# Converting weight pieces from a single load, with the low part made on GpSimd and the first units reordered

## The chip, the cores and the metric

The kernel runs on one core of a Trainium2 chip. The core has a matrix engine (PE, whose weight loads the profile lists apart as PEld), a vector engine (DVE), an activation engine (ACT), GpSimd (POOL) and SyncE (SP), which here issues nearly all transfers. The metric is device time in microseconds (us) of one execution; lower is better. All times below are us unless marked ns.

## The reference

Two stages follow each other. The first is attention with random-feature maps; its output is regrouped to 4608 rows of 512, and a feed-forward layer is applied to it.

```python
def phi(x):                                   # q, k, v: (8, 8, 576, 64); w_phi: (64, 128)
    proj = np.einsum('bhsd,df->bhsf', x, w_phi)
    proj = proj - np.max(np.abs(proj), axis=-1, keepdims=True)
    return np.concatenate([np.exp(proj), np.exp(-proj)], axis=-1)
q_p, k_p = (phi(q), phi(k))
kv = np.einsum('bhsf,bhsd->bhfd', k_p, v)
num = np.einsum('bhsf,bhfd->bhsd', q_p, kv)
den = np.einsum('bhsf,bhf->bhs', q_p, np.sum(k_p, axis=2))[..., None] + 1e-06
...
h = x @ w_in                                  # x: (4608, 512), w_in: (512, 2048)
sp = np.where(h > 20.0, h, np.log1p(np.exp(np.minimum(h, 20.0))))
out = (h * np.tanh(sp)) @ w_out               # w_out: (2048, 512)
```

The two weight matrices `w_in` and `w_out` arrive as 8-byte numbers (float64) and have to be turned into 4-byte ones on the chip.

## The kernel before

**Attention units.** The keys come as 36 units k0, k1, ... and the queries as 36 units q0_0, q0_1, q1_0, ... of 512 columns each. A unit is loaded (`load k0`, tile `raw`), projected on PE (`project`, L360, tiles `pp`), has its absolute maxima taken and subtracted on DVE (`centre`, L364 and L372: two reductions and two subtractions, one of each per half), and goes through the exponential on ACT. A key unit is then summed against the values `v` on PE (`sum`, L401, tiles `kvps`). A query unit is first turned (`dt`, L480, in its first three groups by PE), multiplied with the key sums (`num`, L401), divided on DVE (`divide`, L523 to L525, three instructions), turned back (`xt`, L545) and split into a high and a low part (`xTh` on ACT, `xTl` on DVE).

**Feed-forward.** For each group c of 256 rows PE multiplies `x` with `w_in` (`in c f`, L575, tiles `h`), ACT applies the nonlinearity, and PE multiplies with `w_out` (`out c f`, L610, tiles `o`; from the fifth group on in a form with fewer products, L745). Each product is the sum of three, high x high, high x low and low x high, so every weight piece is needed as a high tile and a low tile.

**Weight pieces.** Both matrices are cut into 32 pieces of 128 x 512 numbers, named `("in", i, j)` and `("out", i, 0)`. `win_2_0` is the converted piece ("in", 2, 0). A piece is loaded as raw words (`words`, L256), and a second load (`middle`, L260) brings the same bytes shifted by two bytes, for all but the last three pieces. From the high word ACT takes the magnitude (`abs`, L265). DVE then clamps it (L279), shifts it (L292) and puts back sign and top bits (L297), which gives the high part; from the shifted load it makes the remaining bits (L284) and a power of two (L302), and multiplies the two to the low part (L307). ACT rounds the high part to its final tile (`ready`, L326). So DVE works six instructions on a piece with a shifted load, and seven on one of the last three (L287 and L288 take the place of L284).

**What sets the order.** Every step is a task with an engine, a key, a guessed duration and dependencies. `Plan.order` replays them and so writes down one fixed order for PE, DVE, ACT and SP; each engine then takes its instructions strictly in this order and waits where an input is late. The keys come from tables of numbers at the top (`FIRST_KEYS` and `FIRST_QUERIES` for the first units, `WKEYS` for the weight pieces, E0, E1 and others for the steady stretch). Behind the replay the first loads are rearranged by hand (NLOADS, VLATE, LATER). Transfers share one issue order on SP, and the hardware takes them from there.

The raw words and the finished piece use the same memory: the finished high tile overwrites part of the words.

Of the kernel before, what the change touches and what calls it, by code (L numbers as in the profile page):

```python
# [57 lines left out]
FIRST_KEYS = {0: -15.83, 1: -13.11, 2: -9.97, 3: -9.13, 4: -7.79, 5: 5.39, 6: 7.33, 7: 10.36, 8: 12.26, 9: 26.17, 10: 26.27}  # L58
FIRST_QUERIES = {0: -11.55, 1: -8.5, 2: -1.4, 3: -0.74, 4: 12.74, 5: 12.11}
# [11 lines left out]
WKEYS = [-6.42, -8.84, -5.8, -0.77, 4.55, 2.54, 6.13, 9.34, 4.27, 5.56, 11.66, 11.19, 18.21, 21.9, 23.26, 22.05,  # L71
         25.09, 22.07, 26.7, 34.84, 24.54, 37.47, 32.85, 40.81, 37.93, 41.3, 40.78, 41.2, 43.66, 37.64, 39.51, 45.36]
LAG, TAIL, TAILLAG = 4, 10, 2
TWOH = 10
HFIRST = 0.0
# [4 lines left out]
TLEAD = 3.609  # L80
SPLITC = 12
QFIRST = 99
URGENT = 2.061
UCENTRE = -0.136
# [4 lines left out]
class Plan:  # L89
# [11 lines left out]
    def order(self):  # L101
# [86 lines left out]
        at = [n for n, task in enumerate(tasks) if task["name"].startswith("load ")][:NLOADS]  # L188
        loads = sorted(range(NLOADS), key=lambda i: i + VLATE * tasks[at[i]]["name"].startswith("load v"))
        for n, task in zip(at, [tasks[at[i]] for i in loads]):  # L190
            tasks[n] = task
        moved = [next(task for task in tasks if task["name"] == name) for name in LATER]
        tasks = [task for task in tasks if task["name"] not in LATER]
        at = 1 + next(n for n, task in enumerate(tasks) if task["name"] == LATER_THAN)
        return tasks[:at] + moved + tasks[at:]
# [3 lines left out]
def attention_then_mish(ctx, tc, qT, kT, va, w_phi, w_in, w_out, out):  # L199
# [24 lines left out]
    weight, finished, homes_of, to_add, middles, rests = {}, {}, {}, {}, {}, {}  # L224
# [42 lines left out]
    def parts_of(piece):  # L267
        words = weight[piece].rearrange("p (a b) -> p a b", b=2)
        if piece in middles:
            return words, middles[piece].bitcast(U32).rearrange("p (a b) -> p a b", b=2)  # L270
        if piece not in rests:
            nm = "%s_%d_%d" % piece
            rests[piece] = (scratch(f"rest_{nm}", f"rest:{piece}", U32),
                            work.tile([P, 512], U32, tag="half", name=f"t_{nm}", bufs=NHALF))
        return words, None

# [4 lines left out]
    def split_rest(piece):  # L281
        words, middle = parts_of(piece)
        if middle is not None:
            nc.vector.tensor_scalar(middle[:, :, 0], middle[:, :, 0], 7, None, op0=ALU.logical_shift_left)  # L284
        else:
            rest = rests[piece][0]
            nc.vector.tensor_scalar(rest, words[:, :, 1], 23, None, op0=ALU.logical_shift_left)  # L287
            nc.vector.scalar_tensor_tensor(rest, words[:, :, 0], 9, rest, op0=ALU.logical_shift_right, op1=ALU.bitwise_or)  # L288
# [5 lines left out]
    def split_sign(piece):  # L294
        w = to_add[piece]
        words = weight[piece].rearrange("p (a b) -> p a b", b=2)
        nc.vector.scalar_tensor_tensor(w, words[:, :, 1], 0xC0000000, w, op0=ALU.bitwise_and, op1=ALU.bitwise_or)  # L297

    def split_power(piece):
        words, middle = parts_of(piece)  # L300
        t = rests[piece][1] if middle is None else middle[:, :, 1]
        nc.vector.tensor_scalar(t, to_add[piece], 0xFF800000, None, op0=ALU.bitwise_and)  # L302

    def split_low(piece):
        _, middle = parts_of(piece)
        rest, t = rests[piece] if middle is None else (middle[:, :, 0], middle[:, :, 1])
        nc.vector.scalar_tensor_tensor(both(piece)[1], like(piece, rest), 2.0 ** -43, like(piece, t.bitcast(F32)),  # L307
                                       op0=ALU.mult, op1=ALU.mult)
# [15 lines left out]
    def high_weight(kind, i, j):  # L324
        piece = kind, i, j
        nc.scalar.copy(both(piece)[0], like(piece, to_add.pop(piece).bitcast(F32)))  # L326
# [532 lines left out]
    for t, is_query, n in units:  # L859
# [5 lines left out]
        if not is_query:  # L865
# [12 lines left out]
            for k, (p, parts) in enumerate(mine):  # L878
# [75 lines left out]
    nmiddle = len(pieces) - len(homes)  # L954
    for i, pc in enumerate(pieces):
# [5 lines left out]
        if i < nmiddle:  # L961
            home = homes[i % len(homes)]
            add(f"middle {nm}", "SP", -47.45 + i * 0.1, 0.42, lambda pc=pc, home=home: load_middle(*pc, home),
                deps=last_use.get(home, []), take=[(home, f"m:{nm}")], size=524288)
# [203 lines left out]
```

## Time and profile before

| What | Value |
|---|---|
| Three timed runs | 1046.14 us median (1042.16 to 1047.18) |
| Profiled execution, first to last instruction | 1043.5 us |
| Profiled execution's own time | no figure apart from its span; the median of the runs lies 2.6 us above the span |
| PE busy | 1029.5 us, 99% of the span |
| DVE busy | 738.0 us, 71% |
| ACT busy | 655.6 us, 63% |
| POOL busy | 0.7 us, 6 instructions |
| Moved by transfers | 223.09 MB |

The shares are means over an opening of some 170 us, in which the weights are converted, and a long steady stretch. They differ between the two, so the opening has to be looked at by itself.

### The profile page before, as it was taken

What the parts mean: (1) busy time and instruction counts of PE and PEld (TensorE: products, weight loads), DVE (VectorE), ACT (ScalarE), POOL (GpSimd) and SP (SyncE); (2) the same over time, 40 slices, a digit from 0 to 9 for tenths busy, and PEclk for the clock granted to TensorE, in tenths of its full rate; (3) what the DMA queues carried; (4) which work ended last, traced back from release to release, by engine and by line L of the source; (5) the groups of instructions that cost most, each with busy time, mean ns of one, the idle gap of its engine ahead of it and who ended that gap; (6) DMA issues with size and microseconds to landing.
All of it is one profiled execution on the core that took longest, in us unless ns stands there. A gap on an engine that the chain in (4) does not pass through costs nothing.

```text
span 1043.5 us, 30075 instructions
## 1 busy us (share of the span) xinstructions
PE 1029.5 (99%) x12286; PEld 990.6 (95%) x12286; DVE 738.0 (71%) x1692; ACT 655.6 (63%) x1028; POOL 0.7 (0%) x6
## 2 busy tenths in 40 slices
PE   8999999999999999999999999999999999999998
PEld 7888998899889999999999999999999999999998
DVE  7998998677886675767676767675776666666553
ACT  6799898667665756666666656665665565545532
POOL 0000000000000000000000000000000000000000
PEclk9999999999999999999999999999999999999999
DMA  9768664465977666767667564757576666765844
GB/s 319 271 235 317 189 209 136 125 204 160 296 246 235 212 211 205 222 215 226 216 209 230 193 209 159 242 186 243 175 237 196 206 189 212 219 220 190 291 142 155
DMA packets 158313, 223.09 MB, mean 214 GB/s; under 512 B 17120, under 2 KB 75616, under 8 KB 158176
## 3 DMA queue, kind: packets, MB, share of 16 engines
q1 hardware_dynamic: 158032, 221.11, 64.8%
q8 instruction: 97, 1.59, 0.6%
q14 instruction: 40, 0.33, 0.1%
q10 hardware_dynamic: 144, 0.07, 0.0%
HBM read 177.59 MB, written 43.52 MB: 212 GB/s over the span
## 4 chain that ended last, share of the span: by engine, by line
PE 93%; DVE 3%; DMA 3%; issue 1%; SPq 1%; ACT 0%; DVEq 0%; ACTq 0%
PE h L575 38%; PE oy L745 8%; PE ox L745 8%; PE o L610 8%; PE ow L745 8%; PE num L401 7%; PE kvps L401 6%; PE oz L745 4%; PE pp_q L360 4%; PE pp_k L360 3%; DMA middle_in<-w_in 1%; DMA words_out<-w_out 1%; DMA v<-va 1%; DMA words_in<-w_in 0%; PE dt L480 0%
## 5 line engine op out<-in xcount | busy, mean ns | idle before, releaser
L575 PE MATMUL h<-xTh,win 128*128 128x256 f32 x2304 | 429.1, 280 | 1.0 <-DVE e_k L372 1.0
L575 PEld LDWEIGHTS h<-xTh,win 128*128 128x128 f32 x2304 | 361.0, 188 | 5.2 <-PE h L575 1.2
L575 PE MATMUL h<-xTl,win 128*128 128x256 f32 x1152 | 321.9, 279 | 0.0
L575 PEld LDWEIGHTS h<-xTl,win 128*128 128x128 f32 x1152 | 216.5, 188 | 1.8
L660 DVE TENSOR_TENSOR sl<-s,sh 128x640 fp32r<-128x640 f32 x112 | 92.0, 823 | 106.7 <-ACT sh L656 101.7
L656 ACT CAST sh<-s 128x640 fp32r<-128x640 f32 x112 | 80.7, 722 | 90.8 <-DVE s L651 79.2
L641 ACT ACTIVATE u<-h 128x512 f32<-128x512 f32 x112 | 66.9, 598 | 96.2 <-PE h L575 95.7
L649 DVE TENSOR_TENSOR s<-u 128x256 f32<-128x256 f32 x112 | 46.9, 418 | 90.5 <-ACT u L641 90.3
L401 PEld LDWEIGHTS kvps<-v,e_k 128*64 128x64 f32 x2560 | 78.4, 137 | 9.4 <-issue 4.2
L401 PE MATMUL kvps<-v,e_k 128*64 128x66 f32 x2560 | 84.0, 223 | 3.2 <-issue 2.5
L745 PE MATMUL oy<-wout,sh 128*128 128x256 f32 x448 | 85.7, 284 | 0.0
L745 PE MATMUL ox<-wout,gh 128*128 128x256 f32 x440 | 83.6, 283 | 0.0
L745 PE MATMUL ow<-wout,sh 128*128 128x256 f32 x440 | 82.9, 281 | 0.0
L610 PE MATMUL o<-wout,gh 128*128 128x512 f32 x256 | 81.7, 400 | 0.0
L401 PE MATMUL num<-kv,e_q 128*64 128x66 f32 x2304 | 78.1, 225 | 1.8 <-DVE xTl L559 1.0
L401 PEld LDWEIGHTS num<-kv,e_q 128*64 128x64 f32 x2304 | 73.2, 139 | 4.9 <-issue 1.5
L436 ACT ACT_TABLE_LOAD x25 | 32.1, 1283 | 64.9 <-DVE e_k L372 64.5
L745 PEld LDWEIGHTS oy<-wout,sh 128*128 128x128 f32 x448 | 68.5, 188 | 1.6
L745 PEld LDWEIGHTS ox<-wout,gh 128*128 128x128 f32 x440 | 67.2, 188 | 0.7
L745 PEld LDWEIGHTS ow<-wout,sh 128*128 128x128 f32 x440 | 67.4, 188 | 0.0
L745 PE MATMUL oy<-wout,sl 128*128 128x256 f32 x224 | 62.9, 281 | 0.0
L745 PE MATMUL ow<-wout,sl 128*128 128x256 f32 x220 | 61.7, 280 | 0.0
(120 smaller groups left out, 1824.4 us busy)
## 6 DMA issues: line engine op xcount, KB each, us to landing
wout<-terms SPq DMA_DIRECT2D x344, 256.0 KB, 4.6
there_e<-e_q SPq DMA_DIRECT2D x60, 256.0 KB, 2.6
e_q<-there_e SPq DMA_DIRECT2D x240, 64.0 KB, 2.3
v<-va SPq DMA_DIRECT2D x32, 330.0 KB, 4.8
out<-osb SPq DMA_DIRECT2D x35, 256.0 KB, 2.6
raw_k<-kT SPq DMA_DIRECT2D x34, 256.0 KB, 3.5
raw_q<-qT SPq DMA_DIRECT2D x34, 256.0 KB, 3.5
there_x<-via SPq DMA_DIRECT2D x30, 256.0 KB, 2.0
```

The source lines that it names most:

```text
L360: nc.tensor.matmul(ps[j][:, n], raw[rows, n * P:(n + 1) * P], w_phi2[rows], start=True, stop=True)
L401: nc.tensor.matmul(ps[rows], lhsT[h], rhs[h], start=start, stop=stop, skip_group_check=True)
L436: nc.scalar.activation(e[:, 1, :], e[:, 0, :], AF.Exp)
L575: nc.tensor.matmul(ps, w[:, wcol], x[:, cc % 2, :], start=(n == 0), stop=(n == 11))
L610: nc.tensor.matmul(ps.rearrange("p (k n) -> p k n", k=2), g[:, cols], w, start=(i == first and k == 0), stop=(i == end and k == 2))
L641: nc.scalar.activation(u, h_live.pop((c, fp)).rearrange("p f s -> p (f s)"), AF.Mish)
L649: nc.vector.tensor_tensor(s[:, :CH], u[:, :CH], u[:, CH:], op=ALU.add)
L656: nc.scalar.copy(mix_high[c, fp], mixed[c, fp])
L660: nc.vector.tensor_sub(mix_low[c, fp], mixed.pop((c, fp)), mix_high[c, fp].bitcast(F32))
L745: nc.tensor.matmul(ps, a, b, start=(begins and n == 0 and (apart or not half)), stop=(ends and n == 2), skip_group_check=True)
```

## The change

The second, shifted load is gone (29 transfers of 511.5 KB), and with it L284, L302 and L307 on DVE (for the last three pieces also L287 and L288). The high word keeps 9 more bits through the shift, and one new DVE instruction, `tail`, adds the top three bits of the low word. ACT then rounds this fuller number to the high tile, and GpSimd subtracts the high tile from the fuller number, which gives the low tile. DVE is left with four instructions for a piece. GpSimd's instructions are now ordered by the plan too. The key tables and the steady stretch's numbers are others, the hand-made rearrangement of loads is removed, and a dependency keeps the sums of a pair of heads in the order of their units.

```diff
-EARLY = 2.042
+EARLY = 1.984
-SOONER = 1.5
+SOONER = 1.602
-FIRST_KEYS = {0: -15.83, 1: -13.11, 2: -9.97, 3: -9.13, 4: -7.79, 5: 5.39, 6: 7.33, ...
+FIRST_KEYS = {0: -18.68, 1: -15.48, 2: -11.31, 3: -9.5, 4: -6.98, 5: -5.65, 6: 5.13, ...
-NLOADS = 11
-LATER = ["load ('in', 0, 1)", "load ('out', 0, 0)", "load ('out', 2, 0)", "load ('out', 3, 0)"]
-LATER_THAN = "load v5"
-VLATE = 4.5
-E0 = 0.138
-E1 = 0.171
-GX = 0.403
-ET = 0.107
+E0 = -1.33
+E1 = -1.113
+GX = 0.577
+ET = 0.456
-URGENT = 2.061
-UCENTRE = -0.136
+URGENT = 3.619
+UCENTRE = -1.189
...
-    def load_middle(kind, i, j, home):
-        middle = middles[kind, i, j] = slot_tile(home, U16, f"middle_{kind}_{i}_{j}", 2048)
-        in_parts(middle[:, :2046], octets(kind, i, j).bitcast(U16)[:, 1:2047])
...
-    def split_rest(piece):
...
     def split_shift(piece):
         w = to_add[piece]
-        nc.vector.tensor_scalar(w, w, 3, 0x3FFFF000, op0=ALU.logical_shift_left, op1=ALU.bitwise_and)
+        nc.vector.tensor_scalar(w, w, 3, 0x3FFFFFF8, op0=ALU.logical_shift_left, op1=ALU.bitwise_and)
...
+    def split_or(piece, half, scalar, op):
         w = to_add[piece]
         words = weight[piece].rearrange("p (a b) -> p a b", b=2)
+        nc.vector.scalar_tensor_tensor(w, words[:, :, half], scalar, w, op0=op, op1=ALU.bitwise_or)
+    def split_sign(piece):
+        split_or(piece, 1, 0xC0000000, ALU.bitwise_and)
+    def split_tail(piece):
+        split_or(piece, 0, 29, ALU.logical_shift_right)
     def split_low(piece):
-        nc.vector.scalar_tensor_tensor(both(piece)[1], like(piece, rest), 2.0 ** -43, like(piece, t.bitcast(F32)),
-                                       op0=ALU.mult, op1=ALU.mult)
+        hi, lo = both(piece)
+        nc.gpsimd.tensor_sub(lo, like(piece, to_add.pop(piece).bitcast(F32)), hi.bitcast(F32))
...
-        split("power", 0.34, split_power, [f"sign {nm}", f"rest {nm}" if own else f"middle {nm}"])
-        split("split", 0.61, split_low, [f"power {nm}", f"rest {nm}"], ...
+        split("tail", 0.61, split_tail, [f"sign {nm}"])
+        add(f"ready {nm}", "ACT", WKEYS[i] + 0.1, 0.55, lambda pc=pc: high_weight(*pc), deps=[f"tail {nm}"])
+        add(f"split {nm}", "POOL", WKEYS[i] + 0.2, 1.4, lambda pc=pc: split_low(pc), deps=[f"ready {nm}"], give=[f"u:{nm}", f"w:{nm}"])
```

Line numbers shift with the edit: in the changed kernel L317 loads a unit (L352 before), L396 loads `v` (L431), L240 loads a piece (L251), L254, L258 and L263 are the clamp, the shift, and the two instructions `sign` and `tail` (L279, L292, L297), and L273 is the subtraction.

**SP, the start of the program.** These are the first transfers that SP issues before the change; a `raw` tile holds two units, so the first three rows are units k0, k1 and q0_0.

```order
L352 DMA raw_k0_89<-kT 128x128 x4
L352 DMA raw_k0_89<-kT 128x512
L352 DMA raw_q0_0_95<-qT 128x512
L352 DMA raw_q0_0_95<-kT 128x512
L431 DMA v_0_98<-va 128x660
```

The same place in the changed kernel:

```order
L317 DMA raw_k0_89<-kT 128x128 x4
L396 DMA v_0_94<-va 128x660
L317 DMA raw_k0_89<-kT 128x512
L396 DMA v_1_97<-va 128x660
L317 DMA raw_q0_0_99<-qT 128x512
```

The value tiles v_0 and v_1 have moved ahead of units k1 and q0_0, so that k1 has one more transfer in front of it and q0_0 two.

**DVE, ahead of the first feed-forward product.** Before the change these rows are the end of the work on piece ("in", 3, 0), the last of the four pieces that the first `in` needs, with the centring of query unit q1_1 and the division of q1_0 around it.

```order
L284 TENSOR_SCALAR middle_in_3_0_508<-middle_in_3_0_508 128x512
L297 SCALAR_TENSOR_TENSOR w_in_3_0_629<-words_in_3_0_159,w_in_3_0_629 128x512
L559 TENSOR_TENSOR xTl_0_1_725<-xt_0_1_707,xTh_0_1_715 128x512
L302 TENSOR_SCALAR middle_in_3_0_508<-w_in_3_0_629 128x512
L364 TENSOR_REDUCE m0_q1_1_730<-pp0_q1_1_611 128x4
L364 TENSOR_REDUCE m1_q1_1_732<-pp1_q1_1_612 128x4
L372 TENSOR_TENSOR e0_q1_1_734<-pp0_q1_1_611,m0_q1_1_730 128x512
L372 TENSOR_TENSOR e1_q1_1_736<-pp1_q1_1_612,m1_q1_1_732 128x512
L307 SCALAR_TENSOR_TENSOR win_3_0_738<-middle_in_3_0_508 128x512
L523 TENSOR_SCALAR r0_1_0_785<-num0_1_0_740 128x4
```

In the changed kernel the last of these four pieces is ("in", 2, 0); L254 is its clamp, L258 its shift, and the two L263 rows are sign and tail.

```order
L254 TENSOR_SCALAR w_in_2_0_619<-w_in_2_0_619 128x512
L436 COPY kv_4_733<-kvps_4_646 128x264
L258 TENSOR_SCALAR w_in_2_0_619<-w_in_2_0_619 128x512
L254 TENSOR_SCALAR w_out_0_0_692<-w_out_0_0_692 128x512
L263 SCALAR_TENSOR_TENSOR w_in_2_0_619<-words_in_2_0_125,w_in_2_0_619 128x512
L524 TENSOR_TENSOR xTl_0_1_756<-xt_0_1_724,xTh_0_1_740 128x512
L263 SCALAR_TENSOR_TENSOR w_in_2_0_619<-words_in_2_0_125,w_in_2_0_619 128x512
L258 TENSOR_SCALAR w_out_0_0_692<-w_out_0_0_692 128x512
```

The rows on `middle` and the multiplication into `win` are gone from DVE, the piece's fourth and last step is a second L263, and steps of ("out", 0, 0) stand between them; the centring of q1_1 follows behind these rows. The subtraction that ends the piece is no longer here: GpSimd, which had nothing behind the identity matrix at the start, now has 32 rows L273, one for each piece, each behind ACT's rounding of its piece.

**PE, behind the products of query unit q0_1.** Before the change the first half of q0_1's `num` is followed by the projections of q1_0 and q1_1 (rows that repeat are left out).

```order
L401 MATMUL num0_0_1_568<-kv_2_565,e0_q0_1_348 64x66 x4
L401 MATMUL num0_0_1_568<-kv_2_565,e1_q0_1_350 64x66 x4
L360 MATMUL pp0_q1_0_596<-w_phi2_80,raw_k4_105 128x128
L360 MATMUL pp1_q1_0_597<-w_phi2_80,raw_k4_105 128x128
L360 MATMUL pp0_q1_1_611<-w_phi2_80,raw_q1_1_196 128x128
L360 MATMUL pp1_q1_1_612<-w_phi2_80,raw_q1_1_196 128x128
```

In the changed kernel the same `num` is followed by the projection of key unit k5, and those of q1_0 and q1_1 come behind it.

```order
L366 MATMUL num0_0_1_542<-kv_2_536,e0_q0_1_348 64x66 x4
L366 MATMUL num0_0_1_542<-kv_2_536,e1_q0_1_350 64x66 x4
L325 MATMUL pp0_k5_563<-w_phi2_80,raw_k4_155 128x128
L325 MATMUL pp1_k5_564<-w_phi2_80,raw_k4_155 128x128
L325 MATMUL pp0_q1_0_583<-w_phi2_80,raw_q1_0_197 128x128
L325 MATMUL pp1_q1_0_584<-w_phi2_80,raw_q1_0_197 128x128
```

The projection of k5, and behind it the sums of k5 (80 products in the trace's count), have moved ahead of the first feed-forward product; before the change both stand behind the fourth.

## Rows read from the trace of the kernel before

**Rows 1.** Page, part 1: busy time, share of the span, instructions of each engine.

```profile
PE 1029.5 (99%) x12286; PEld 990.6 (95%) x12286; DVE 738.0 (71%) x1692; ACT 655.6 (63%) x1028; POOL 0.7 (0%) x6
```

**Rows 2.** Windows: length, busy time by engine (instructions), PE's granted clock, DMA share, GB/s.

```profile
0.00:46.69 46.69, 40.00 (x747) 36.74 (x747) 38.08 (x85) 30.39 (x63) 0.70 (x6) 0.96 0.88 308
0.00:73.75 73.75, 65.47 (x1123) 60.40 (x1123) 63.79 (x143) 55.44 (x102) 0.70 (x6) 0.98 0.79 273
0.00:100.00 100.00, 91.52 (x1360) 82.79 (x1362) 87.73 (x198) 80.20 (x153) 0.70 (x6) 0.98 0.82 284
170.00:1000.00 830.00, 827.89 (x9832) 804.36 (x9832) 566.74 (x1301) 501.99 (x761) 0.00 (x0) 1.00 0.66 212
```

**Rows 3.** Timeline, DVE: start, length, line, operation, count, idle time before.

```profile
5.17 1.29 DVE L364 TENSOR_REDUCE m_k<-pp_k 128x4 f32<-128x512 f32 x2 [5.17 <-PE pp_k L360]
6.37 1.28 DVE L372 TENSOR_TENSOR e_k<-pp_k,m_k 128x512 f32<-128x512 f32 x2
...
18.27 0.43 DVE L284 TENSOR_SCALAR middle_in<-middle_in 128x512 uint32<-128x512 uint32 x1 [1.46 <-DMA middle_in<-w_in]
...
23.15 0.42 DVE L279 TENSOR_SCALAR w_in<-w_in 128x512 f32<-128x512 f32 x1
23.48 0.42 DVE L284 TENSOR_SCALAR middle_in<-middle_in 128x512 uint32<-128x512 uint32 x1
...
27.30 1.29 DVE L307 SCALAR_TENSOR_TENSOR win<-middle_in 128x512 fp32r<-128x512 uint32 x2
28.51 0.68 DVE L364 TENSOR_REDUCE m_k<-pp_k 128x4 f32<-128x512 f32 x1
...
44.61 0.15 DVE L523 TENSOR_SCALAR r<-num 128x4 f32<-128x4 f32 x1
...
45.35 0.42 DVE L279 TENSOR_SCALAR w_out<-w_out 128x512 f32<-128x512 f32 x1
```

**Rows 4.** Timeline, PE: the opening's products that the sum counts.

```profile
5.70 2.08 PE L360 MATMUL pp_k<-w_phi,raw_k 64*128 64x128 f32 x16 [0.57 <-DMA raw_k<-kT]
...
26.69 1.16 PE L360 MATMUL pp_k<-w_phi,raw_k 64*128 64x128 f32 x16
...
28.37 2.56 PE L401 MATMUL kvps<-v,e_k 128*64 128x66 f32 x80
30.76 1.11 PE L401 MATMUL num<-kv,e_q 128*64 128x66 f32 x32
...
40.68 0.60 PE L401 MATMUL num<-kv,e_q 128*64 128x66 f32 x6 [0.98 <-DVE xTl L559]
...
46.25 0.60 PE L480 MATMUL dt<-ident,e_q 128*128 128x128 f32 x4
...
46.69 0.60 PE L545 MATMUL xt<-ident,x 128*128 128x128 f32 x4
...
73.75 0.73 PE L610 MATMUL o<-wout,gh 128*128 128x512 f32 x2
```

**Rows 5.** Chain that ended last: start, length, engine, tile, line, count.

```profile
205.74 2.80 PE o L610 x12
```

**Rows 6.** Groups by line, ACT and POOL: count, busy, mean ns, idle before.

```profile
L326 ACT CAST win<-w_in 128x512 fp32r<-128x512 f32 x16 | 9.9, 626 | 1.4 <-DVE w_in L297 1.4
masks.py:199 POOL TENSOR_SCALAR_AFFINE_SELECT ident<-ident 128x128 f32<-128x128 f32 x1 | 0.3, 294 | 0.1
L641 ACT ACT_TABLE_LOAD x45 | 57.7, 1283 | 0.8
```

**Rows 7.** Windows again: the stretch of the slower clock, and the first loads.

```profile
40.00:45.00 5.00, 4.32 (x70) 4.19 (x71) 4.87 (x13) 2.49 (x5) 0.00 (x0) 0.66 1.01 385
...
4.00:6.00 2.00, 1.43 (x14) 1.14 (x12) 0.83 (x2) 0.00 (x0) 0.00 (x0) 1.00 0.97 316
```

More of the change, by code (lines that the diff above doesn't have):

```diff
@@ L187, in order @@
         tasks = [task for _, _, task in issued]
[L188 to L195, printed above, removed]
+        return tasks
 @with_exitstack
@@ L223, in attention_then_mish @@
     pieces += [("out", 12 + i, 0) for i in range(4)]
-    weight, finished, homes_of, to_add, middles, rests = {}, {}, {}, {}, {}, {}
+    weight, finished, homes_of, to_add = {}, {}, {}, {}
     slots = [f"w{kind}_{i}_{j}" for kind, i, j in pieces]
@@ L265, in magnitude @@
         nc.scalar.activation(w.bitcast(F32), high.bitcast(F32), AF.Abs)
[L267 to L275, printed above, removed]
     def split_clamp(piece):
@@ L957, in attention_then_mish @@
         ahead = [f"split {pieces[i - NAHEAD]}"] if i >= NAHEAD else []
-        used = [f"split {pieces[n]}" for n in range(nmiddle) if homes[n % len(homes)] == slot]
         add(f"load {nm}", "SP", -47.5 + i * 0.1, 0.42, lambda pc=pc: load_weight(*pc),
-            deps=last_use.get(slot, []) + used, after=ahead, take=[(slot, f"w:{nm}")], size=524288)
[L961 to L964, printed above, removed]
+            deps=last_use.get(slot, []), after=ahead, take=[(slot, f"w:{nm}")], size=524288)
         add(f"abs {nm}", "ACT", WKEYS[i] - 0.5, 0.55, lambda pc=pc: magnitude(*pc), deps=[f"load {nm}"], take=[("w", f"u:{nm}"), ("part", f"w:{nm}")])
@@ L967, in split @@
             add(f"{step} {nm}", "DVE", WKEYS[i], took, lambda pc=pc, fn=fn: fn(pc), deps=deps, late=0.13, **more)
-        own = i >= nmiddle
         split("clamp", 0.34, split_clamp, [f"abs {nm}"])
-        split("rest", 0.95 if own else 0.34, split_rest, [f"load {nm}" if own else f"middle {nm}"],
-              take=[("part", f"rest:{nm}"), ("half", f"t:{nm}")] if own else [])
         split("shift", 0.34, split_shift, [f"clamp {nm}"])
         split("sign", 0.61, split_sign, [f"shift {nm}"])
-        split("power", 0.34, split_power, [f"sign {nm}", f"rest {nm}" if own else f"middle {nm}"])
-        split("split", 0.61, split_low, [f"power {nm}", f"rest {nm}"], give=[f"rest:{nm}", f"t:{nm}"] if own else [f"m:{nm}"])
-        add(f"ready {nm}", "ACT", WKEYS[i] + 0.1, 0.55, lambda pc=pc: high_weight(*pc), deps=[f"sign {nm}", f"power {nm}"], give=[f"u:{nm}", f"w:{nm}"])
+        split("tail", 0.61, split_tail, [f"sign {nm}"])
+        add(f"ready {nm}", "ACT", WKEYS[i] + 0.1, 0.55, lambda pc=pc: high_weight(*pc), deps=[f"tail {nm}"])
+        add(f"split {nm}", "POOL", WKEYS[i] + 0.2, 1.4, lambda pc=pc: split_low(pc), deps=[f"ready {nm}"], give=[f"u:{nm}", f"w:{nm}"])
     tiles = [(c, f) for part in range(2) for c in range(2) for f in range(4 * part, 4 * part + 4)]
@@ L1127, in attention_then_mish @@
                         give=[f"osb{tt}:{c}"], size=262144)
-    with tc.manual_schedule(engines={mybir.EngineType.PE, mybir.EngineType.DVE, mybir.EngineType.Activation, mybir.EngineType.SP}):
+    with tc.manual_schedule(engines={mybir.EngineType.PE, mybir.EngineType.DVE, mybir.EngineType.Activation, mybir.EngineType.SP, mybir.EngineType.Pool}):
         trial = bank("att", [P, P], "trial")
```

32 lines of the change are left out of this document (8 added, 24 removed).

## The prediction

> **What bounds the kernel now.** I read the page first: PE is busy for 1029.5 of 1043.5 us [rows 1], and the change gives it neither more nor fewer products, so only PE's idle or slowed time can be won or lost. The windows then show where that time lies. In the first 100 us PE stands for 8.5 us, while from 170 to 1000 us it stands for 2.1 us [rows 2]; the rest is the end of the program. So the opening counts. There DVE is busy for 87.7 of 100 us and has its first work only at 5.17 [rows 2, 3], which makes it the engine that PE and ACT wait for most. PE's row at 40.68 shows it: 0.98 us of idle time that a DVE instruction ended [rows 4], and behind it a granted clock of 0.66 over 5 us, a mean over full speed (2.4 GHz) and half (1.2 GHz), after PE had stood [rows 7]. That alone is 1.7 us of full speed lost. Before it, at 18.27, DVE itself stood for 1.46 us for a shifted load [rows 3].
>
> **How I count.** In the opening PE follows DVE closely. So I take two points of PE's order and add up DVE's own work before each, in the old order and in the new one. DVE's prices are distances from start to start: a reduction or a subtraction over 512 columns 0.60 (two take 5.17 to 6.37), a one-input weight instruction 0.33 (23.15 to 23.48), a two-input one 0.60 (two take 27.30 to 28.51), a division, three instructions, 0.74 (44.61 to 45.35) [rows 3]; a query unit has two divisions. Copies and 256-column subtractions go at 0.33, the `xTl` at 0.60.
>
> **Point one: the turning back of q1_0, on PE at 46.69 [rows 4].** Before, DVE has 34 reductions and subtractions, 17 short instructions, 10 long ones, six divisions and some tiny ones ahead: 20.4 + 5.6 + 6.0 + 4.4 + 0.4 = 36.8. It starts at 5.17 and is past the last division at 45.35 [rows 3], so it stood for 3.4 us. In the new order it is 38 reductions and subtractions (unit k5 came in), 12 short ones, 10 long ones, six divisions: 22.8 + 4.0 + 6.0 + 4.4 + 0.4 = 37.6, or 0.8 more. Of the 3.4 us the wait of 1.46 at the shifted load goes. On the other side k1, which PE waited for until 5.70 [rows 4], now has v_0 (128 x 660 numbers, 0.34 MB) ahead of it; at 316 GB/s [rows 7] that is 1.1 us later, and DVE, which starts on k1's projection, shifts with it. So 3.0 us are left, and DVE is through at 5.17 + 37.6 + 3.0 = 45.8, plus four times c, where c is the time that one GpSimd subtraction takes from DVE. At this point PE has more behind it than before: the projection of k5 (1.16), its 80 sum products (28.37 to 30.76, 2.39), and one turning less (46.25 to 46.69, 0.44) [rows 4], together 3.1 us. The gain here is 46.69 - 45.8 + 3.1 - 4c = 4.0 - 4c.
>
> **Point two: the output products that need several converted `w_out` pieces, on PE at 73.75 [rows 4].** Up to here DVE was busy for 63.8 us before, so it stood for 73.75 - 5.17 - 63.8 = 4.8 us [rows 2]. In the new order piece ("out", 1, 0) is the late one. Ahead of its last DVE step and with it are 46 reductions and subtractions, 25 short ones, 21 long ones, eight divisions: 27.6 + 8.2 + 12.6 + 5.9 + 0.4 = 54.7. By the same prices the old order has 46, 48, 23 and eight, or 27.6 + 15.8 + 13.8 + 5.9 + 0.4 = 63.5, which agrees with the busy 63.8. The 8.8 us between them are 21 short and two long weight instructions and two other short ones. I leave 3.7 us of idle time: the 4.8 less the shifted load's 1.46, plus k1's 1.1, less 0.7 for steps on shifted loads that no longer wait. That gives 5.17 + 54.7 + 3.7 = 63.6 on DVE. Behind it follow ACT's rounding (0.63), the subtraction and two hand-overs of some 0.1. No row shows a subtraction on GpSimd. Its nearest row is the 128 x 128 select of 0.294 us [rows 6], four times that is 1.18 us for 512 columns. So the piece is ready at 65.6 + 9c, since nine subtractions lie ahead. PE has by then one projection less (1.16), 64 sum and `num` products more (1.9) and six output products less (2.80 for 12 [rows 5], so 1.4) behind it, together 0.7 less. The gain is 73.75 - 65.6 - 0.7 - 9c, or 7.4 - 9c.
>
> **The price c.** Two ends: 0, if GpSimd works beside DVE, and 1.18, if DVE stands for the whole length of each. No row of this trace shows GpSimd and DVE at work together, so nothing between is measured. I take 0.2, near the low end, since the two engines have their own queues here and DVE has other idle time (4.8 us up to the second point) in which part of a standstill would fall. That makes the gain 3.2 at the first point and 5.6 at the second. The first point isn't the end of it: before, PE stands for another 1.6 us between the two (46.69 - 40.00 against 73.75 - 65.47 [rows 2]), plus the slower products in between, and the new order has DVE ahead there. So I take the second, 5.6 us.
>
> The Trainium skill's page "SBUF — State Buffer", section "Who interferes with whom", speaks against this: it says that DVE and GpSimd share one pair of ports as an exclusive lock, that a DVE instruction in a two-port mode or with two SBUF inputs stands until a reading GpSimd instruction has ended, and the other way round. The Trainium skill's page "GPSIMD Engine Reference", section "Performance versus the Vector engine", gives 4497 ns for a two-input addition over 2048 columns, from which I estimate 1.12 us for 512; with c at that estimate the second point's sum would be 7.4 - 10.1, or 2.7 us slower. No run here shows either yet.
>
> **Other parts.** The 29 shifted loads of 511.5 KB leave the queue, 14.8 MB of what was moved in the opening at 284 GB/s [rows 2]; beyond the wait priced above I count nothing for it, since the raw units and pieces wait little elsewhere. A buffer for the fuller number is held for some 2 us longer, until the subtraction is done; the magnitude of a later piece on ACT can wait for it, and ACT's idle time (16.3 us up to 46.69 [rows 2]) covers that; uncovered it would cost the same 2 us once. The new order has ten more activation-table loads on ACT (146 for 136), 1.28 us each [rows 6], most of them in the steady stretch, where ACT is busy for 502 of 830 us [rows 2]; its idle 328 us cover 12.8. Uncovered, they would cost up to 12.8.
>
> **Sum.** 1043.5 - 5.6 = 1037.9 for a profiled execution. The median of the runs shown lies 2.6 above that span, so 1046.1 - 5.6 = 1040.5.
>
> **Rivals.** First, a standstill of DVE for most of a subtraction, c from 0.5 to 1.4. For it speaks that DVE is the fullest engine of the opening [rows 2]; against it that no wait of this kind has been seen. The second point gives 7.4 - 4.5 to 7.4 - 12.6, that is 1043.2 to 1051.3; it is level at c = 0.82. By the lock that the Trainium skill states the time comes out here, near 1049.
>
> Second, the side of slower: the same place with c above 1.4, where 7.4 - 9c passes -5.2. It needs subtractions longer than the bound from the select, which has one input where the subtraction has two; at twice the bound (2.36) it is 14 us slower, 1060.
>
> Third, the opening's gain is given back later: the retuned order lets table loads and late exponentials through to PE. A third of the 12.8 us is 4.3, so 1045. Against it stands that PE's 2.1 us of idle time over 830 us shows how much slack there is [rows 2].
>
> Fourth, DVE's saving doesn't help, because PE in the opening waits for loads or for ACT: then only k1's delay of 1.1 us is left, 1047.
>
> **How the numbers follow.** The forecast (c below 0.5) gets 0.55, the first rival 0.2, the second 0.08, the third 0.1, the fourth 0.07. About 0.5% (5.2 us) is what a measurement of this kernel can tell from no change. Of the forecast 0.39 lies beyond 5.2 us, since the steady stretch can add up to 2.1, and 0.16 within; the first rival gives 0.15 within and 0.05 slower; the second 0.08 slower; the third 0.05 faster (a retuned stretch that gains instead), 0.04 within, 0.01 slower; the fourth 0.06 within, 0.01 slower. That makes faster 0.44, same 0.41, slower 0.15. The range goes from c = 0 with the steady 2.1 us won (1046.1 - 7.4 - 2.1 = 1036.6) to c at 1.18 (1046.1 + 3.2 = 1049.3). The likeliest case alone, c from 0 to 0.5, has 1038.7 to 1043.2.
>
> **What would show it.** The first `h` product should start near 46 us with k5's sums done; PE's idle time up to 100 us should fall from 8.5 to about 4; the start-to-start distances of DVE's weight instructions (0.33 and 0.60) should stay. The prediction is wrong if these grow while a POOL subtraction runs, if a POOL row is far over 1.2 us, if PE waits for POOL at L575 or L610, or if PE's idle time after 170 us exceeds 5 us.

## The result, and the profile after

The changed kernel is slower by 1.1%: 1054.99 us median (1054.54 to 1057.16, four runs) against 1044.21 (1042.16 to 1047.18, four runs), a ratio of 1.0106 with a 95% interval of 1.0082 to 1.0130. The forecast was 1040.5, with 1049.3 as its upper end. The profiled execution's span is 1052.8 us, 9.3 more than before.

The page's first part (engine, busy us, share, instructions) and the windows of the changed kernel (columns as in [rows 2]: length, busy time of PE, PEld, DVE, ACT and POOL with their instructions, granted clock, DMA share, GB/s):

```profile
PE 1033.3 (98%) x12286; PEld 990.6 (94%) x12286; DVE 734.1 (70%) x1625; ACT 669.9 (64%) x1038; POOL 45.8 (4%) x38
```

```profile
0.00:73.75 73.75, 65.58 (x1167) 59.88 (x1168) 64.04 (x125) 51.46 (x100) 14.40 (x16) 1.00 0.59 199
0.00:100.00 100.00, 90.67 (x1420) 81.68 (x1421) 87.28 (x167) 74.73 (x151) 21.98 (x21) 1.00 0.63 213
100.00:190.00 90.00, 86.78 (x867) 77.03 (x866) 71.61 (x135) 70.96 (x110) 23.85 (x17) 1.00 0.26 84
190.00:1000.00 810.00, 806.53 (x9585) 782.73 (x9585) 551.40 (x1267) 508.61 (x752) 0.00 (x0) 1.00 0.66 211
```

Up to 73.75 us DVE is as busy as before, 64.0 against 63.8 us [rows 2], although it has far fewer instructions, 125 against 143. PE stands for 9.3 us in the first 100, where 8.5 were to fall to 4, and for 3.2 us more from 100 to 190. In the kernel before the last two windows read:

```profile
100.00:190.00 90.00, 90.00 (x1007) 81.61 (x1006) 79.44 (x180) 73.44 (x115) 0.00 (x0) 1.00 0.54 180
190.00:1000.00 810.00, 807.89 (x9586) 786.34 (x9586) 551.36 (x1267) 489.86 (x741) 0.00 (x0) 1.00 0.66 214
```

There PE doesn't stand at all from 100 to 190. DVE's groups up to 180 us, and GpSimd's, show where the saved time went (count, busy us, mean ns of one, idle before):

```profile
L263 DVE SCALAR_TENSOR_TENSOR w_in<-words_in,w_in 128x512 uint32<-128x512 uint32 x32 | 26.1, 816 | 0.3
L263 DVE SCALAR_TENSOR_TENSOR w_out<-words_out,w_out 128x512 uint32<-128x512 uint32 x31 | 23.9, 779 | 0.5
L557 DVE TENSOR_TENSOR gl<-u,gh 128x256 fp32r<-128x256 f32 x32 | 16.2, 545 | 1.6 <-ACT gh L549 1.3
L329 DVE TENSOR_REDUCE m_k<-pp_k 128x4 f32<-128x512 f32 x20 | 12.8, 679 | 6.5 <-PE pp_k L325 6.5
L254 DVE TENSOR_SCALAR w_out<-w_out 128x512 f32<-128x512 f32 x16 | 9.2, 572 | 8.4 <-ACT w_out L250 8.3
L258 DVE TENSOR_SCALAR w_in<-w_in 128x512 uint32<-128x512 uint32 x16 | 8.6, 538 | 0.2
L258 DVE TENSOR_SCALAR w_out<-w_out 128x512 uint32<-128x512 uint32 x16 | 7.6, 481 | 0.2
L254 DVE TENSOR_SCALAR w_in<-w_in 128x512 f32<-128x512 f32 x16 | 7.3, 457 | 1.0 <-ACT w_in L250 1.0
```

```profile
L273 POOL TENSOR_TENSOR win<-w_in,win 128x512 fp32r<-128x512 f32 x16 | 23.2, 1449 | 78.7 <-ACT win L291 78.7
L273 POOL TENSOR_TENSOR wout<-w_out,wout 128x512 fp32r<-128x512 f32 x16 | 22.2, 1388 | 58.8 <-ACT wout L291 58.8
```

The reduction L329 reads PSUM (PE's result buffers), and it takes what it took before, 0.68 us [rows 3]. Everything that DVE does on weights, and the `gl` (the low part of the nonlinearity's result), got longer: in the kernel before these took 0.42 us with one input or with 256 columns, and 0.685 with two inputs over 512. The timeline at two places (start, length) shows how:

```profile
32.50 1.28 POOL L273 TENSOR_TENSOR win<-w_in,win 128x512 fp32r<-128x512 f32 x1 [31.20 <-ACT win L291]
32.51 0.42 DVE L490 TENSOR_TENSOR x<-num,r 128x256 f32<-128x256 f32 x1
32.85 1.22 DVE L258 TENSOR_SCALAR w_in<-w_in 128x512 uint32<-128x512 uint32 x1
...
162.08 1.47 POOL L273 TENSOR_TENSOR wout<-w_out,wout 128x512 fp32r<-128x512 f32 x1 [1.72 <-ACT wout L291]
162.35 1.82 DVE L557 TENSOR_TENSOR gl<-u,gh 128x256 fp32r<-128x256 f32 x2
```

L490 starts beside the subtraction, reads `num` from PSUM and takes 0.42 us, as in the kernel before. L258 starts behind it, works within SBUF (`w_in` to `w_in`), and isn't through until the subtraction is (34.07 against 33.78). I call this a standstill of DVE. At 162 us the first of two `gl` does the same, and PE's rows show who was waiting for it:

```profile
6.50 2.08 PE L325 MATMUL pp_k<-w_phi,raw_k 64*128 64x128 f32 x16 [1.30 <-DMA raw_k<-kT]
9.31 2.08 PE L325 MATMUL pp_q<-w_phi,raw_q 64*128 64x128 f32 x16 [0.73 <-DMA raw_q<-qT]
...
14.09 2.09 PE L366 MATMUL kvps<-v,e_k 128*64 128x66 f32 x64
...
46.49 0.38 PE L540 MATMUL h<-xTh,win 128*128 128x256 f32 x1
...
48.62 0.41 PE L510 MATMUL xt<-ident,x 128*128 128x128 f32 x2
...
73.00 0.73 PE L575 MATMUL o<-wout,gh 128*128 128x512 f32 x2
...
161.80 0.63 PE L575 MATMUL o<-wout,gh 128*128 128x512 f32 x2
163.89 0.50 PE L575 MATMUL o<-wout,gl 128*128 128x512 f32 x1 [1.46 <-DVE gl L557]
...
183.99 0.50 PE L575 MATMUL o<-wout,gh 128*128 128x512 f32 x1 [0.60 <-POOL wout L273]
```

Three things differ from [rows 4]. k1's projection starts at 6.50 instead of 5.70. The products of point two start at 73.00, hardly earlier than 73.75, though the first `in` product is at 46.49, near the 46 that was said. And PE now waits behind 100 us, for a `gl` that stood and for a late low tile.

To compare kernels whose orders differ I use one figure throughout, **PE's lag**. I add up PE's own work in the order of its matmul records (without the trial products at the start), each at its usual distance from start to start (0.0355 us for `sum` and `num`, 0.0655 projection, 0.1095 turning, 0.117 `in` products and the late output form, 0.2335 `out`), and take that sum from the time at which the next record starts. The lag is what PE has lost so far, to standing and to the slower clock alike.

| Kernel | behind 8 us of work | 32 | 65 | 105 | 190 | 1000 |
|---|---|---|---|---|---|---|
| before | 6.2 | 12.1 | 14.3 | 15.0 | 14.9 | 14.9 |
| changed | 8.8 | 8.7 | 13.8 | 15.8 | 20.5 | 24.1 |
| e5 changed, fill instead of subtraction | 8.1 | 7.5 | 10.5 | 11.0 | 11.4 | 17.3 |
| e6 before, new steady numbers | 6.2 | 9.9 | 12.2 | 12.4 | 13.7 | 17.9 |
| e7 changed, units first | 6.0 | 6.1 | 12.7 | 13.3 | 18.1 | 23.5 |
| e9 e7 and old steady numbers | 6.0 | 7.0 | 12.0 | 14.1 | 18.9 | 19.7 |
| e10 e9 with the fill | 6.1 | 5.9 | 9.0 | 9.5 | 9.6 | 10.8 |
| e11 before, with fills | 6.0 | 11.0 | 13.2 | 13.4 | 13.3 | 13.7 |
| e13 e9, 13 subtractions beside centring | 6.1 | 5.7 | 9.4 | 13.3 | 21.2 | 22.2 |
| e14 e9, six early ones beside centring | 6.0 | 6.0 | 9.7 | 11.7 | 16.5 | 17.9 |

The changed kernel starts 2.6 us worse, is 3.4 better at 32 us of work, has lost most of that at 65 (1.5 of it right behind 32), and loses 6.7 between 65 and 190 and 3.6 behind it.

### The profile page after: what moved, and what is told of

It reads as the page before. It is cut to its first block, busy times and chain, and to the rows that moved or that the text cites. A ratio compares the mean times of both kernels' runs of the same rounds, so it can differ in the third digit from the quotient of the medians.

```text
span 1052.8 us, 30074 instructions
## 1 busy us (share of the span) xinstructions
PE 1033.3 (98%) x12286; PEld 990.6 (94%) x12286; DVE 734.1 (70%) x1625; ACT 669.9 (64%) x1038; POOL 45.8 (4%) x38
## 4 chain that ended last, share of the span: by engine, by line
PE 80%; DVE 11%; ACT 4%; issue 3%; DMA 1%; SPq 1%; POOL 0%; POOLq 0%; ACTq 0%; DVEq 0%
PE h L540 33%; PE oy L710 7%; PE ox L710 7%; PE ow L710 7%; PE num L366 6%; PE kvps L366 5%; PE o L575 5%; PE oz L710 3%; PE pp_q L325 3%; PE pp_k L325 3%; DVE w_in L263 1%; DVE w_out L263 1%; DVE gl L557 1%; DVE m_k L329 1%; DVE e_k L337 1%
```

## The experiments

Each kernel was timed in the same rounds as the kernel before, whose median there was 1044.4 to 1045.1 us.

| Run | us median | ratio to before, 95% interval |
|---|---|---|
| e1 before, plus 32 subtractions | 1058.70 | 1.0098 to 1.0151 |
| e11 before, plus 32 fills | 1044.24 | 0.9991 to 1.0010 |
| e2 changed, subtraction on DVE | 1054.60 | 1.0064 to 1.0110 |
| e5 changed, fill | 1047.68 | 1.0014 to 1.0040 |
| e3 conversion alone, old tables | 1064.77 | 1.0148 to 1.0215 |
| e8 e3 with the fill | 1057.49 | 1.0089 to 1.0142 |
| e4 changed, old steady numbers | 1052.75 | 1.0051 to 1.0091 |
| e6 before, new steady numbers | 1049.84 | 1.0037 to 1.0067 |
| e7 changed, units first | 1053.48 | 1.0051 to 1.0103 |
| e9 units first, old steady numbers | 1050.83 | 1.0049 to 1.0079 |
| e10 e9 with the fill | 1041.80 | 0.9964 to 0.9982 |
| e12 e9 without tail | 1043.70 | 0.9979 to 1.0002 |
| e13 e9, 13 beside centring | 1053.26 | 1.0074 to 1.0108 |
| e14 e9, six beside centring | 1048.15 | 1.0019 to 1.0043 |
| e15 e14, late ones on DVE | 1049.04 | 1.0026 to 1.0056 |

**Is it GpSimd's subtraction? (e1, e11)** The kernel before gets GpSimd work and nothing else; GpSimd joins the engines whose order is fixed.

```diff
-        nc.scalar.copy(both(piece)[0], like(piece, to_add.pop(piece).bitcast(F32)))
+        w = like(piece, to_add.pop(piece).bitcast(F32))
+        nc.scalar.copy(both(piece)[0], w)
+        nc.gpsimd.tensor_sub(w, w, both(piece)[0].bitcast(F32))   # e11: nc.gpsimd.memset(w, 0.0)
...
```

> The kernel before, with everything in its old order, and one added GpSimd subtraction behind each of the 32 castings of the high part (it reads the fuller number and the high tile and writes over the fuller number, which nothing reads afterwards). It leaves nothing of the computation out. Theory A (standstill: a GpSimd subtraction of 512 columns takes some 0.5 us from DVE): DVE's weight and gl instructions in the first 180 us get longer, by 12 to 20 us in all, PE's idle time up to 100 us grows from 8.5 to 12 or more, and the time is 1048 to 1052 against 1044. Theory B (the retuned tables and the start made the changed kernel slow, GpSimd's work costs nothing that PE sees): DVE's instructions may be longer, but the time stays at 1043 to 1045.

> The kernel before with one added GpSimd instruction for each piece, at the same place as the added subtraction of the first experiment, which only fills the buffer of the fuller number (nothing reads it afterwards) and so reads nothing. It leaves nothing of the computation out. It holds the buffer, as the subtraction did, but for a shorter time. If the standstill made the first experiment slow: 1044 to 1047. If it was the held buffer (ACT waited 8.2 us for GpSimd there) or any GpSimd work at all: 1050 or more.

The subtractions alone make the kernel before 14 us slower, more than the 1048 to 1052 expected; the fills at the same place cost nothing. In e1's trace ACT also waits for the buffer that the subtraction holds (waits of ACT up to 170 us: total, times, longest), which the changed kernel's ACT never does:

```profile
ACT w_out L265 <- POOL w_in L328: 4.4, 3, 2.4
ACT w_in L265 <- POOL w_in L328: 3.8, 2, 3.2
```

With the fills one such wait of 0.7 us is left. The subtractions hold the buffer for so long because DVE can also keep GpSimd out:

```profile
81.81 9.62 POOL L328 TENSOR_TENSOR w_in<-w_in,win 128x512 f32<-128x512 f32 x2 [5.05 <-DVE w_in L292]
```

The first of these two subtractions takes 8.4 us. DVE has 17 instructions within SBUF behind one another up to 89.0 us, none of them longer than usual, and the subtraction is done 1.2 us after the last. So e1 holds two costs, the standstill and the buffer, which isn't split further; e11 shows that work on GpSimd that reads nothing is free here.

**The same in the changed kernel (e2, e5).** The order of all instructions stays; only the subtraction's engine, or what it does, is changed.

```diff
-        nc.gpsimd.tensor_sub(lo, like(piece, to_add.pop(piece).bitcast(F32)), hi.bitcast(F32))
+        nc.vector.tensor_sub(lo, like(piece, to_add.pop(piece).bitcast(F32)), hi.bitcast(F32))   # e2
+        to_add.pop(piece); nc.gpsimd.memset(lo.bitcast(F32), 0.0)                                # e5
```

> The changed kernel with every instruction in its place, only that the 32 subtractions are DVE's instead of GpSimd's. Theory A (standstill): DVE gets 32 x 0.60 = 19 us more work and loses some 17 us of standstill, so the time stays within 2 us of 1055; the weight instructions fall back to 0.42 and 0.68 us of busy time. Theory B (GpSimd's work is free for DVE): DVE has 19 us more in an opening in which it is the fullest engine, so 1060 or more.

> The changed kernel in its own order, only that GpSimd fills the low tile with zeros in place of the subtraction, so it writes 512 columns and reads nothing. It leaves out the low part of the weights. Theory A (a reading GpSimd instruction makes DVE stand): DVE's sign and tail fall from 0.80 to 0.685 us, its clamp and shift to 0.42 and gl to 0.42, PE's 1.5 us of idle time at 162 us goes, and the time is 1046 to 1051. Theory B (the tables and the start made it slow): 1053 to 1056.

Both came out as the standstill has it. Groups of DVE and GpSimd over the whole execution, e2 first, then e5:

```profile
L263 DVE SCALAR_TENSOR_TENSOR w_in<-words_in,w_in 128x512 uint32<-128x512 uint32 x32 | 21.9, 685 | 0.3
L557 DVE TENSOR_TENSOR gl<-u,gh 128x256 fp32r<-128x256 f32 x64 | 24.2, 418 | 11.1 <-ACT gh L549 10.7
L258 DVE TENSOR_SCALAR w_in<-w_in 128x512 uint32<-128x512 uint32 x16 | 6.7, 421 | 0.2
L273 DVE TENSOR_TENSOR win<-w_in,win 128x512 fp32r<-128x512 f32 x16 | 10.9, 684 | 0.7 <-ACT win L291 0.7
```

```profile
L263 DVE SCALAR_TENSOR_TENSOR w_in<-words_in,w_in 128x512 uint32<-128x512 uint32 x32 | 21.9, 684 | 0.3
L258 DVE TENSOR_SCALAR w_in<-w_in 128x512 uint32<-128x512 uint32 x16 | 7.7, 481 | 0.2
L274 POOL MEMSET win<- 128x512 f32 x16 | 10.0, 630 | 84.5 <-DVE w_in L263 57.1 <-PE o L576 7.2 <-issue 7.1
```

With e2's lengths (0.685 and 0.688 for L263, 0.418 for `gl`, 0.419 to 0.423 for L254 and L258) the changed kernel's stretch is 32 x 0.131 + 31 x 0.091 + 32 x 0.127 + 16 x (0.151 + 0.117 + 0.058 + 0.038) = 16.9 us, or c = 16.9 / 32 = 0.53 us. That is nearly the 0.60 that DVE takes for the subtraction itself, and so e2 and the changed kernel run alike. Without the reading the changed kernel gains 7.3 us. (A fill also doesn't wait for ACT's rounding, so the low tiles are ready sooner; e12 below bears on that.) Only some one-input instructions are still a little longer in e5, beside fills.

**The tables (e3, e8, e4, e6, e7).** e3 has the conversion with all old numbers and the old rearrangement of loads, e8 the same with the fill. e4 takes the old steady numbers (EARLY, SOONER, E0, E1, GX, ET, TLEAD, HFIRST, URGENT, UCENTRE) into the changed kernel, e6 the new ones into the kernel before. e7 puts back the part of the rearrangement that keeps `v` behind the first units:

```diff
+        at = [n for n, task in enumerate(tasks) if task["name"].startswith("load ")][:11]
+        loads = sorted(range(11), key=lambda i: i + 4.5 * tasks[at[i]]["name"].startswith("load v"))
+        for n, task in zip(at, [tasks[at[i]] for i in loads]):
+            tasks[n] = task
         return tasks
```

> The changed kernel's conversion (one load for a piece, sign and tail on DVE, subtraction on GpSimd) with the old tables: the old keys of units and pieces, the old rearrangement of the first loads, the old numbers of the steady stretch. Theory A (standstill takes 0.5 us for each subtraction): the saved seven or eight microseconds of DVE's work up to 74 us shrink to 7.4 - 9 x 0.53 = 2.6, so 1041 to 1044. Theory B (the tables made it slow, the conversion gives what was forecast): 1037 to 1040. A third case: the old tables do not suit the new dependencies, and it is slower than 1046.

> The conversion from a single load on the old tables, and GpSimd fills the low tile with zeros in place of the subtraction; it leaves out the low part of the weights. This is the case that the forecast priced with c = 0. Theory A (the standstill makes the conversion slow): 1037 to 1042, so over 20 us below the same kernel with the subtraction. Theory C (the old tables do not suit the new dependencies, whatever GpSimd does): 1055 to 1064.

> The changed kernel with the old EARLY, SOONER, E0, E1, GX, ET, HFIRST, TLEAD, URGENT and UCENTRE; the order of units and pieces at the start stays new. Theory B1 (the retuned steady stretch gives time away): PE's idle time from 170 to 1000 us falls back from some 7 to 2 or 3 us, so 1049 to 1051. Theory A1 (the steady stretch lost little, the loss lies in the first 200 us): 1053 to 1056.

> The kernel before with the new EARLY, SOONER, E0, E1, GX, ET, HFIRST, TLEAD, URGENT and UCENTRE, nothing else changed. If these numbers cost by themselves what putting the old ones back gained (2.2 us), it is 1046 to 1049; if they suit only the new opening and cost nothing here, within 1 us of 1044.8; if they are bad for a stretch that the old opening reaches earlier, above 1050.

> The changed kernel with the first eleven unit, value and weight loads rearranged as before: units k1, q0_0 and k2 ahead of v_0, k3 ahead of v_1. If the start costs what its trace shows (the first sum product 2.6 us later than before), 1052 to 1053.5; k1's projection comes back from 6.50 to about 5.7 and k0's first sum from 14.1 to below 12. If the opening's later waits swallow it, 1054.5 to 1055.5.

In e3 and e8 neither the standstill alone nor the tables alone gave the time; the case written down for old tables that don't suit came out in both. With old tables the new conversion is 20 us slower, and 13 without the reading, so those tables don't fit the new dependencies. Which of their numbers doesn't isn't settled; but the standstill is worth 7.3 us here too. e4 falls between its two ranges, 2.2 us better. e6 is 5.4 slower than the kernel before, more than the 1 to 4 expected: the new steady numbers cost by themselves. Its lag grows by 4.2 behind 190 us of work, where that of the kernel before stays, and in the changed kernel it grows by 3.6. The table loads ahead of the late exponentials are 53 in the changed kernel, 55 in e6, and 45 in the kernel before [rows 6] and in e9. The changed kernel's row:

```profile
L606 ACT ACT_TABLE_LOAD x53 | 68.0, 1283 | 1.0
```

No single wait carries these 4 us. PE's longest behind 190 us in the changed kernel are 1.0 for a centred unit (L337), which the kernel before has too, and 0.6; that the loads are the cause wasn't tried by itself. e7 does what was expected, 1.5 us, and its PE rows show the start of the kernel before again:

```profile
5.42 1.16 PE L329 MATMUL pp_k<-w_phi,raw_k 64*128 64x128 f32 x16 [0.29 <-DMA raw_k<-kT]
...
11.24 2.09 PE L370 MATMUL kvps<-v,e_k 128*64 128x66 f32 x64
```

**All together (e9, e10, e12).** e9 joins e7's rearrangement and e4's numbers. e10 is e9 with the fill. In e12 `split_tail` issues nothing.

> The changed kernel with both the units-first rearrangement of the first loads and the old numbers of the steady stretch; the conversion with GpSimd's subtraction stays. If the parts add up: 1055.0 - 1.5 - 2.2 = 1051.3, so 1050 to 1052.5. If the standstill were not the main loss it would come down to 1046 or less.

> The kernel of the run before this one (units first, old steady numbers), with GpSimd filling the low tile with zeros in place of the subtraction; it leaves out the low part of the weights. This is the forecast's own case, c = 0, no later start, no worse steady stretch. If the forecast's sum of DVE's work was right, the gain against the kernel before is 5 to 8 us: 1037 to 1040. If the saved work on DVE is worth less to PE than summed: 1041 to 1044. Against the run before this one the standstill then costs 8 to 13 us.

> Units first, old steady numbers, GpSimd's subtraction kept, but DVE's 32 tail instructions left out in their places: the last three bits of the fuller number are zero. DVE has 32 x 0.60 = 19 us less work in the first 180 us, about as much as the standstills take (17.4 us). If DVE's time is what counts, whatever takes it, this comes out within 3 us of the run that fills with zeros; if the standstill hurts through its place (gl, which PE waits for at once), 3 us or more above it.

The parts add up: 1055.0, 1053.5, 1050.8, and with the reading gone 1041.8. The last step, 9.0 us, is the largest. The order of the steps matters, though: with the reading taken out first (e5) it is worth 7.3 us, and start and numbers together are then worth 5.9 (e5 against e10) instead of 4.2.

e12 gives DVE back about as much time in another place (32 x 0.60 us), and keeps GpSimd's subtraction and its wait for ACT. It lands 1.9 us above e10, and most of that is the granted clock: its four executions at a mean of 1.000 took 1041.8 to 1042.2 us and its six at 0.998 took 1043.7 to 1044.9, while nine of e10's ten are at 1.000, with a median of 1041.9. So what counts is DVE's time, whatever takes it, and that the fill has its low tiles ready sooner is worth little. Windows of e10:

```profile
0.00:73.75 73.75, 69.10 (x1206) 63.09 (x1208) 64.84 (x136) 56.58 (x110) 8.31 (x18) 1.00 0.64 222
...
100.00:190.00 90.00, 90.00 (x887) 80.56 (x886) 69.92 (x145) 69.19 (x109) 8.95 (x15) 1.00 0.23 75
190.00:1000.00 810.00, 807.13 (x9588) 786.05 (x9588) 546.83 (x1259) 486.13 (x736) 0.00 (x0) 1.00 0.66 213
```

PE stands for 4.65 us up to 73.75, where the kernel before stands for 8.28 [rows 2], and not at all from 100 to 190. This is the forecast's own case, and it is 3.2 us better than the kernel before, not 5.6 or more. At a granted clock of 1.000 the kernel before has a median of 1043.8 us (30 of its 65 executions in these rounds, three far longer ones left out), so 1.9 of the 3.2 are left between executions at that clock.

**Fixed price, or a matter of what runs beside it? (e13, e14, e15)** A low tile's subtraction is kept back until DVE is past the first reduction of a centring, and runs beside the other three instructions, which read PSUM. It isn't kept back further once its product or its buffer is needed.

```diff
     def centre_max(unit, j):
...
+        if j == 0:
+            subtract(m=m)      # for what is pending: copy m[:, :1] on GpSimd, then tensor_sub
```

> Units first, old steady numbers, the whole computation. Of the 32 GpSimd subtractions, 15 wait until DVE is past the first of the four instructions that centre a unit (by a copy of one column of its maxima), so that they run beside DVE instructions that read PSUM; the others run as before, where their product or buffer is needed sooner. If only DVE instructions that read and write SBUF stand beside a subtraction, the standstills fall from 17 us to 8 to 11 and the time from 1050.8 to 1045 to 1048. If every subtraction takes its half microsecond from DVE wherever it lies, or the later low tiles hold PE up, it stays at 1050 or above.

> As the run before this one, but only subtractions of the first 75 us (by the order's own clock) wait for a centring, six of them; all later ones run as soon as their casting is done. Up to some 75 us PE should be as far as when all early ones wait (2.6 us ahead of the kernel without waiting); PE's four waits for GpSimd (7.1 us) go, and the later standstills come back. If the place beside centring is what helps and the lateness is what hurt: 1047 to 1049. If waiting for a centring gains nothing: 1050 or more.

> As e14, with the 21 subtractions behind 75 us on DVE at 0.60 us each instead of on GpSimd. The standstills of that part (about 13 us by the overlaps) go and 12.6 us of own work come in their place, without GpSimd's 1.3 us ahead of the product that needs the piece, so the same as e14 or up to 2 us less: 1045.5 to 1048. If DVE's place in the order suffers (it now waits for ACT's casting), 1049 or more.

e13's timeline of DVE and GpSimd:

```profile
30.91 1.28 DVE L346 TENSOR_REDUCE m_k<-pp_k 128x4 f32<-128x512 f32 x2
31.66 0.18 POOL L286 COPY gate<-m_k 128x1 f32<-128x1 f32 x1 [30.36 <-DVE m_k L346]
31.80 1.28 POOL L288 TENSOR_TENSOR win<-w_in,win 128x512 fp32r<-128x512 f32 x1
32.11 1.28 DVE L356 TENSOR_TENSOR e_k<-pp_k,m_k 128x512 f32<-128x512 f32 x2
33.30 0.68 DVE L271 SCALAR_TENSOR_TENSOR w_in<-words_in,w_in 128x512 uint32<-128x512 uint32 x1
```

The whole subtraction runs beside DVE, and none of the DVE rows is longer than without it. The trace has 13 copies into `gate`, so 13 subtractions waited, not the 15 expected. Behind 65 us of work e13 is 2.6 us ahead of e9, nearly at e10. Behind that it loses all of it, since tiles come late (waits of PE up to 200 us):

```profile
PE h L560 <- POOL win L288: 7.1, 4, 3.4
```

e14 waits for a centring only early, with six subtractions, keeps the gain, and is 2.7 us faster than e9: so it is the neighbour that sets the price. It is the fastest version here that computes everything with the new conversion, and still 3.2 us slower than the kernel before. e15 came out at its second case (1049 or more) and is no better than e14: its `split` on DVE waits for ACT's casting, and PE once waits 2.5 us for such a tile.

## Why the prediction was wrong

Two steps of the sum failed: the price c of a subtraction, and the count that ended at point two. With the measured c the sum at point two would still be 7.4 - 4.8, or 2.6 us faster; it is the uncounted part that makes the kernel slower.

**The price c** is the step that failed first. It took 0.2 us, because the engines have their own queues and a standstill could fall into DVE's idle time. Measured are 0.53, because 20 of the 32 subtractions in the timeline meet a DVE instruction that works within SBUF, and that one stands until the subtraction ends: 0.42 became 1.22 at 32.85 us. For each of these 20 that is 16.9 / 20 = 0.85 us, more than DVE takes for a subtraction of its own; the other 12 cost nothing. The upper bound of the subtraction's length, 1.18 from the select, was too low as well: 1.28 alone, 1.42 on average. With 0.53 a piece saves DVE no more than 0.13 us: it loses four short and two long instructions and gets two of each, 2 x 0.33 = 0.66, less 0.53.

The Trainium skill's page "SBUF — State Buffer", section "Who interferes with whom", was the rule that spoke against the change, and the traces agree with it: two-input instructions within SBUF stood, and one-input ones on weights too; readers of PSUM did not (0.68 us for the centring beside a subtraction), and a GpSimd fill, which only writes, left the two-input ones at 0.684. Its lock should have been the main case, not the first rival.

**The count of subtractions** failed too, and cost more. I let the sum end at point two, with nine subtractions ahead of it, and counted nothing for the 23 behind. From 65 to 190 us of work e9 loses 6.9 us and e10 0.6: two thirds of the standstill's 9.0 us lie there. The kernel before has no idle PE time from 100 to 190 us, and the prediction is silent on that stretch, in which any late `gl` or tile makes PE stand (1.46 us at 163.89, 0.60 at 183.99).

**The gain at the two points** was right in sign and too large. Point one, the turning back of q1_0, starts at 48.62 where 46.69 was before; with the 3.1 us of products that PE now has done by then, that is a gain of 1.2 us, where 3.2 was said. PE's lag there says 1.6 (10.6 against 12.2 us; the 3.4 at 32 us of work has halved two microseconds of work later). Even that isn't there in every execution of the old order: e6 has the same order up to there, but not the slower clock at 40 to 45 us [rows 7], and its lag at this place is 10.2. Point two was to give 5.6 and gave 0.5 at 65 us of work. Even without any standstill and with the old start, where the sum would be 7.4 + 1.1 = 8.5, e10 gives 5.3 there, and less against e11, which has the old order too and lags by 13.2: 4.2.

The premise behind it, that PE follows DVE closely in the opening, isn't what the waits show. The waits of PE up to 73.75 us in the kernel before (total, times, longest; "issue" is time in which PE waited for nothing that the profile shows; the four longest) are

```profile
PE kvps L401 <- issue: 2.5, 2, 1.6
PE trial L1132 <- POOL ident masks.py:199: 1.4, 1, 1.4
PE xt L545 <- DVE x L525: 1.2, 1, 1.2
PE num L401 <- DVE xTl L559: 1.0, 1, 1.0
```

With one more of 0.2 us, DVE's instructions ended 2.4 of PE's 8.3 us of idle time, and in e10 0.6 of 4.65. The sum gave DVE's whole lead to PE, but PE hadn't that much to win, and DVE's further lead buys nothing.

**The start** was put at 1.1 us for k1. PE's rows of the kernel before for q0_0 and the first sum are

```profile
7.57 1.92 PE L360 MATMUL pp_q<-w_phi,raw_q 64*128 64x128 f32 x16
...
11.50 2.09 PE L401 MATMUL kvps<-v,e_k 128*64 128x66 f32 x64
```

so q0_0 came 1.7 us later and the first sum 2.6, where k1's 0.8 (5.70 to 6.50) is below the 1.1. I counted one transfer ahead of k1, but q0_0 has two. In the kernel before, too, k1's projection takes 2.08 us, where e7's takes 1.16; why isn't shown, the granted clock is 1.00 in all three. The start is worth 1.5 us of the time (e7).

**The steady stretch** was the third rival with a chance of 0.1 and 4.3 us; it is real, 2.2 to 2.7 us by the times of e4 and of e9 against e7. **Ten more table loads** were priced at nothing behind ACT's idle time; whether they are what costs there stays open. The buffer held for longer cost nothing in the changed kernel, as said.

Against the forecast, 1040.5, the runs give: standstill 9.0, steady numbers 2.7 and start 1.5 above e10's 1041.8. That e10 comes so near the forecast is partly luck: the forecast started from 1046.14, the median of three runs, where the fourth brings the same kernel to 1044.21, so its 5.6 us would have led to 1038.6.

## What to carry to other kernels

In this kernel, moving an elementwise step that reads SBUF from DVE to GpSimd saved DVE's time only where DVE was idle or read PSUM meanwhile; beside work within SBUF, DVE paid 0.85 us for a step of 0.60, and over all 32 nearly the whole step (0.53). Price such a move over all its instructions, not up to the first point that looks critical, and cap a gain on the feeding engine by the idle time that the fed engine has to give back. A table of numbers that was fitted to one order of work is a change of its own: time it by itself before crediting or blaming the code beside it.

## What the runs showed of the hardware

A GpSimd subtraction of two 128 x 512 tiles took 1.27 to 1.30 us undisturbed, and up to 2.30 in the changed kernel where DVE was at work first: the standstill goes both ways. GpSimd didn't get its turn between DVE instructions that follow each other within SBUF, 17 of them and 8.4 us in e1. GpSimd's fill of 512 columns took 0.52 us at the shortest and 0.6 on average in e5, and made only some one-input DVE instructions within SBUF longer (0.481 against 0.421 on average for L258 on `w_in`), not those with two inputs (0.684). And the granted clock of 0.66 from 40 to 45 us in the profile of the kernel before is there in e11 too, but not in e6, which has the same order up to then, the same wait of 1.0 us for `xTl`, and 1.00 over its first 46.69 us. Its lag is 1.0 us smaller at 28 us of work, ahead of that stretch, and 2.2 at 32, so the slower clock cost 1.2 us, not the 1.7 read from the window. The timed executions of the kernel before differ likewise: the 30 at a mean granted clock of 1.000 have a median of 1043.8 us, the 35 at 0.996 to 0.999 one of 1045.2. So the same short wait of PE was followed by a slower clock in one execution and not in another, at a price of 1.2 to 1.4 us.
